# Linear attention, then a Fourier feed-forward: the first batch's loads, normalisation and the planner's durations rearranged

## The chip, the cores and the metric

The kernel runs on one core of a Trainium2 chip. The metric is device time in microseconds (us), the median of several executions. All data is 32-bit floating point; products that need the full width are made of three matmuls on a high and a low part.

## What is computed

There are 8 batches, 8 heads, 576 tokens and a head dimension of 64. The reference, cut to what matters:

```python
kv  = einsum('bhsd,bhse->bhde', k, v)
out = einsum('bhsd,bhde->bhse', q, kv)
out = out / sqrt(mean(out*out, -1) + 1e-6) * g_norm
x = out.transpose(0, 2, 1, 3).reshape(8, 576, 512)
u = x + real(fft(fft(x, axis=1), axis=2))
un = (u - mean(u)) / sqrt(var(u) + 1e-6)
return u + maximum(un @ w_ch1, 0) @ w_ch2     # 512 -> 2048 -> 512
```

The weights arrive as 64-bit numbers and are turned into pairs of 32-bit numbers on the chip.

## The kernel before, in words

The work is recorded as operations of a planner (class `Plan`), one after another, each with an engine, a duration in nanoseconds (its cost), a rank, the operations that it comes after, and the buffers that it needs. `Plan.run` plays this list against its own clock: of the ready operations on a free engine it emits the one with the lowest rank whose buffers are there. The order of emission becomes the order of the instructions on each engine, apart from a scheduler below it that moves instructions again. On the chip every engine takes its instructions strictly in that order. So a duration in the planner is no time on the chip, but it decides what stands behind what.

For every batch the plan holds these steps, and the names used in this document are theirs:

- **KV** (`plan_kv`, L441): keys and values are loaded by pairs of heads, 256 KB each for keys and values (`km`, `vm`, L460), with one remainder of 128 KB each (`kr`, `vr`, L469). Each pair costs 10 matmuls (L481). The ring `kv` holds 6 such tiles, so the fourth pair waits until the first pair's matmuls have released theirs.
- **QT** (`plan_q_load`, L497, and `plan_q`): the queries of a batch come in two loads of 576 KB (`qt`, L504: side 0 for the tokens of the first half, side 1 for the second half in mirrored order), and are transposed, 4 matmuls for each of 6 groups (L529). The token rows fall into three classes t = 0, 1, 2 (position modulo 3); class t needs a group of each side.
- **OUT** (`plan_out`): 16 matmuls per class (L554), then on ScalarE (ACT) a copy to `x` (L569) and a square (L574), on VectorE (DVE) a sum (L578), on GpSimd (POOL) a multiplication by `g_norm` (L589).
- **Inverse roots** (`plan_y`, L596): once per batch, for all three classes, a square root on ACT (L607), a reciprocal on DVE (L614), three refining steps on POOL (L618 to L620), a last product on DVE (L623).
- **Fold** (`plan_fold`, L632): on each class two multiplications by the inverse root (L651, DVE), one folding addition (L662, DVE), two on POOL (L669), a high part on ACT (L675) and a low part on POOL (L678). Its two work tiles `ab` and `xe` come from the ring `e2` with 4 places.
- **SEQ** (36 matmuls, L693), **CHN** (36, L727) and **TURN** (24 transposes, L813): the two Fourier steps as matmuls, with mixing on ACT, DVE and POOL between them, and the transposed result `unTh`, `unTl` (L822, L825).
- **F1** and **F2** (`plan_early`, L888; L354 and L372): the feed-forward. A block has 512 tokens. While the batches are prepared, F1 and F2 of the blocks that are ready fill TensorE (PE), with the first three of 16 chunks of the weights. An F1 of one chunk is 12 matmuls.
- **Weights** (`plan_w`, L835): one 512 KB load per chunk (`raw`, L282), a clearing step on ACT (L285), five bit steps on DVE (L292 to L302), a sum (L857), for the first matrix also a reduction (L307), a matmul for the mean (L315) and a subtraction (L319), then a high and a low part.

Everything is loaded by SyncE (SP), except the values of the first batch, whose loads are issued by ACT. At most eight loads are in flight: each load waits for the completion of the one eight places ahead of it (the semaphores `DMAHW0` to `DMAHW7` are handed out in turn). A load that waits holds up all that stand behind it on SP.

When the plan is finished, the remaining chunks and blocks follow in a loop that the change does not touch; there the order of PE's instructions is the same in both kernels.

## Time and profile before

| | us |
|---|---|
| median of 3 runs (1024.54 to 1029.22) | 1024.72 |
| the profiled execution | 1026.22 |
| its span, first to last instruction | 1024.4 |
| PE busy | 993.9 |
| DVE busy | 472.0 |
| ACT busy | 322.4 |
| POOL busy | 320.6 |

The profiled execution's time is 1.8 us above its span, and 1.5 us above the median. "Busy" is the time in which an engine works on an instruction; a load of weights into PE (PEld) overlaps its matmuls. PE is busy for 97% of the span, so the time left for it to lose or win is in the gaps and in how long one matmul takes. A row of a timeline shows the start and the length of a group of like instructions, and in brackets how long the engine was idle before it and what ended that.

### The profile page before, as it was taken

The page shows a single profiled execution, that of the slowest core. Times are in us where ns is not written, and L with a number is a line of the kernel's source. Part 1 is how long each engine was busy: PE and PEld are TensorE (multiplying, and loading weights), DVE is VectorE, ACT ScalarE, POOL GpSimd, SP SyncE. Part 2 cuts the span into 40 slices and gives each one's busy share as a digit, 9 for nine tenths or more (in the row PEclk, how much of TensorE's full clock was granted, in tenths as well). Part 3 has the DMA queues.
Part 4 walks back from the last instruction along what each step waited for, and adds up shares of the span by engine and source line. Part 5 has one row for each costly group of instructions (what it writes and reads, how often), then busy time and mean ns, then how long its engine had stood idle before and what let it go on. Part 6 is the DMA issues. An engine that isn't in the chain of part 4 may idle for free.

```text
span 1024.4 us, 15026 instructions
## 1 busy us (share of the span) xinstructions
PE 993.9 (97%) x5866; PEld 839.4 (82%) x5866; DVE 472.0 (46%) x838; ACT 322.4 (31%) x655; POOL 320.6 (31%) x332
## 2 busy tenths in 40 slices
PE   4698999999999999999999999999999999999998
PEld 4697898889888888888888888888888888888886
DVE  4758775654588689998131314131221311311211
ACT  2456565555545434334221212021121021210110
POOL 0555876864865131225722303020020010110000
PEclk9998999999999999999999999999999999999999
DMA  9979979663246766645552515140320400400101
GB/s 245 253 164 280 190 214 263 168 182 139 88 162 212 275 206 253 228 136 175 155 177 74 182 51 170 71 139 1 125 81 0 165 21 1 164 1 1 42 1 41
DMA packets 109194, 140.70 MB, mean 137 GB/s; under 512 B 51790, under 2 KB 76418, under 8 KB 104516
## 3 DMA queue, kind: packets, MB, share of 16 engines
q1 hardware_dynamic: 105588, 132.28, 42.4%
q0 software_dynamic: 1920, 6.29, 2.0%
q10 hardware_dynamic: 1616, 1.18, 0.4%
q8 instruction: 46, 0.75, 0.3%
q14 instruction: 24, 0.20, 0.1%
HBM read 88.33 MB, written 51.40 MB: 136 GB/s over the span
## 4 chain that ended last, share of the span: by engine, by line
PE 93%; DMA 2%; DVE 2%; SPq 1%; issue 1%; ACT 0%; POOL 0%; DVEq 0%; ACTq 0%; POOLq 0%
PE ps_h L354 38%; PE acc L372 38%; PE ps_o L554 4%; PE ps_f L727 3%; PE ps_f L693 3%; PE ps_k L481 3%; PE ps_q L529 2%; PE ps_t L813 2%; DMA vm<-in_v_dram 2%; DVE x L651 1%; DMA qt<-in_q_dram 1%; SPq L510 1%; PE ps_w L315 0%; SPq L460 0%; DVE unTl L825 0%
## 5 line engine op out<-in xcount | busy, mean ns | idle before, releaser
L354 PE MATMUL ps_h<-unTh,w 128*128 128x512 f32 x1152 | 357.1, 391 | 0.0
L372 PE MATMUL acc<-w,hh 128*128 128x512 f32 x1152 | 345.0, 391 | 0.2 <-DVE unTl L825 0.2
L367 DVE SCALAR_TENSOR_TENSOR hl<-ps_h,hh 128x512 fp32r<-128x512 f32 x144 | 99.2, 689 | 379.8 <-ACT hh L364 377.5
L354 PEld LDWEIGHTS ps_h<-unTh,w 128*128 128x128 f32 x1152 | 215.4, 188 | 44.0
L372 PEld LDWEIGHTS acc<-w,hh 128*128 128x128 f32 x1152 | 214.9, 188 | 44.3 <-issue 0.3
L364 ACT ACTIVATE hh<-ps_h 128x512 fp32r<-128x512 f32 x144 | 85.9, 597 | 472.1 <-PE ps_h L354 442.9
L354 PE MATMUL ps_h<-unTl,w 128*128 128x512 f32 x576 | 224.5, 390 | 0.0
L372 PE MATMUL acc<-w,hl 128*128 128x512 f32 x576 | 213.1, 390 | 0.0
L354 PEld LDWEIGHTS ps_h<-unTl,w 128*128 128x128 f32 x576 | 108.3, 188 | 22.7
L372 PEld LDWEIGHTS acc<-w,hl 128*128 128x128 f32 x576 | 107.9, 188 | 22.5
L1133 POOL DMA_INDIRECT uu<-u_scr,rowidx x24 | 23.4, 974 | 286.2 <-DVE uu L1186 175.6
L589 POOL TENSOR_TENSOR x<-x,gb 96x512 f32<-96x512 f32 (+1 forms) x48 | 61.9, 1308 | 55.2 <-ACT x L569 40.6
L1152 POOL TENSOR_TENSOR uu<-uu,up 128x512 f32<-128x512 f32 x36 | 45.7, 1293 | 44.5 <-ACT up L1149 44.5
L554 PEld LDWEIGHTS ps_o<-kvt,fq 64*96 64x96 f32 (+1 forms) x768 | 42.7, 185 | 5.6 <-issue 3.2
L554 PE MATMUL ps_o<-kvt,fq 64*96 64x64 f32 (+1 forms) x768 | 47.0, 274 | 0.3 <-ACT fq L533 0.3
L481 PE MATMUL ps_k<-vm,km 128*64 128x64 f32 x512 | 28.7, 261 | 17.6 <-DMA vm<-in_v_dram 16.7
L1096 POOL TENSOR_TENSOR w<-wap,w 128x512 fp32r<-128x512 f32 x18 | 23.3, 1295 | 70.1 <-ACT w L1095 70.1
L1186 DVE SCALAR_TENSOR_TENSOR uu<-acc,rs_yb,uu 128x512 f32<-128x512 f32 x36 | 25.2, 745 | 42.5 <-PE acc L372 42.5
L578 DVE TENSOR_REDUCE ss<-ps_o 96x8 f32<-96x512 f32 (+1 forms) x48 | 32.2, 682 | 26.2 <-ACT ps_o L574 26.0
L669 POOL TENSOR_TENSOR xe<-ab 96x256 f32<-96x256 f32 (+1 forms) x48 | 37.5, 803 | 19.8 <-DVE ab L662 19.7
L693 PE MATMUL ps_f<-cs,xh 96*128 96x290 f32 (+1 forms) x192 | 41.8, 312 | 0.4 <-DVE x L651 0.4
L481 PEld LDWEIGHTS ps_k<-vm,km 128*64 128x64 f32 x512 | 22.9, 166 | 22.4 <-DMA km<-in_k_dram 16.2
(103 smaller groups left out, 1009.1 us busy)
## 6 DMA issues: line engine op xcount, KB each, us to landing
raw<-in_moe_w_ch_dram SPq DMA_DIRECT2D x32, 512.0 KB, 7.6
qt<-in_q_dram SPq DMA_DIRECT2D x16, 576.0 KB, 9.2
unT_scr<-unTh SPq DMA_DIRECT2D x9, 1024.0 KB
unT_scr<-unTl SPq DMA_DIRECT2D x9, 1024.0 KB, 6.3
part_scr<-part SPq DMA_DIRECT2D x36, 256.0 KB, 4.1
unTh<-unT_scr SPq DMA_DIRECT2D x9, 1024.0 KB, 4.9
...
up<-part_scr SPq DMA_DIRECT2D x36, 256.0 KB, 3.0
```

The source lines that it names most:

```text
L354: nc.tensor.matmul(ps, w[c][:, kc * P : (kc + 1) * P], unT[a][:, kc, :], start=(idx == 0), stop=(idx == 3 * KC - 1),)
L364: nc.scalar.activation(hh, ps, AF.Relu)
L367: nc.vector.scalar_tensor_tensor(hl, ps, 0.0, hh.bitcast(F32), ALU.max, ALU.subtract)
L372: nc.tensor.matmul(acc, hpair[a][:, i * P : (i + 1) * P], w[c], start=(first and n == 0), stop=(last and n == 2),)
L481: nc.tensor.matmul(ps.t[s * D : (s + 1) * D, pr * D : (pr + 1) * D], km[:, s, j, :] if j < 4 else kr[:, h, :], vm[:, s, j, :] if j < 4 els ...
L554: nc.tensor.matmul(pss[s].t[:n, at : at + D], fqs[side].t[half, m, :n], kvt.t[half, m], start=True, stop=True,)
L578: nc.vector.tensor_reduce(ss.t[0][:n, :, t, s::2], pss[s].t[:n].rearrange("p (u m e) -> p u m e", u=2, e=D), AX.X, ALU.add,)
L589: nc.gpsimd.tensor_tensor(v_, v_, gb[:n].unsqueeze(1).to_broadcast([n, H, D]), ALU.mult)
L669: nc.gpsimd.tensor_tensor(o[:, s], a[:, 0], a[:, 1], ALU.subtract if s else ALU.add)
L693: nc.tensor.matmul(ps.t[:, :NS], xs[t].t[a][:n, part, ch * P : (ch + 1) * P], cs[:n, part, c, t, :], start=(idx == 0), stop=(idx == 8),)
L727: nc.tensor.matmul(ps.t[:n, :ND], pt.t[a][:, part, ch, offs[t] : offs[t] + n], cd[:, part, c, ch, :], start=(idx == 0), stop=(idx == 5),)
L1152: nc.gpsimd.tensor_tensor(us[j][i], us[j][i], part, ALU.add)
```

## The change

It does five things, nearly all for the first batch (b == 0).

1. The queries of the first batch come in six loads of 192 KB, by side and class, and each group of transposes waits for its own load only.
2. The inverse roots of the first batch are formed class by class (three times the six small steps, each on a third of the columns), and so class 0 needn't wait for class 2.
3. The last pair of keys and values of the first batch, and the last two pairs of the second, go to tiles of the feed-forward's ring `h`, which stands unused then, rather than to the ring `kv`. The fold of the first batch's class 2 takes its two work tiles from the ring `part`, which stands unused too.
4. The ranks of the weights' loads and conversions are set anew (`W_CONV`, `W_RANK`), so that they come later against the first batch.
5. The planner's durations are set anew: for KV, OUT and the parts of TURN, and every duration of PE counts double until three SEQ groups are done. `pin` ties the instructions that are emitted at the planner's time zero to their order.

The core of the diff, without the functions `pin` and the like:

```diff
+EARLY_KV = (1, 2)
+W_CONV = (4, 5, 6)
+W_RANK = (2, 4, 11)
...
+                    cost = o.cost * (2 if eng == "PE" and cold > 0 else 1)
+                    cold -= o.dense
...
+                if b < 2 and pr >= NPAIR - EARLY_KV[b]:
+                    main = Buf("h", lambda c=c: base.tile(
+                        [P, 2, 4, D], F32, name=c + "m", tag="r", bufs=RINGS["h"]
+                    ))
...
-            mm.append(op("PE", 520, rank(b, KV), go, ld + lds, [ps, kvt] + ts + rest))
+            mm.append(op("PE", 1080, rank(b, KV), go, ld + lds, [ps, kvt] + ts + rest))
...
+        if b == 0:
+            ld = [[dma(
+                240, rank(b, QT) + (2 - j if side else j) / 4,
+                lambda j=j: nc.sync.dma_start(
+                    qt.t[:TR, j].rearrange("p (h d) -> p h d", h=H), src[:, j]
+                ),
+                bufs=[qt],
+            )] for j in range(3)]
...
-        a = op("PE", 900, r, mm, done, [kvt, x, ss] + pss + fqs)
+        a = op("PE", 1540, r, mm, done, [kvt, x, ss] + pss + fqs)
...
-        ab, xe = e2_buf("ab"), e2_buf("xe")
+        if b == 0 and t == 2:
+            ab, xe = (Buf("part", part_tile) for _ in range(2))
+        else:
+            ab, xe = e2_buf("ab"), e2_buf("xe")
...
+        if b == 0:
+            ys = [plan_y(b, ss, reds[t] + [one_row], yp, t) for t in range(3)]
+        else:
+            ys = [plan_y(b, ss, sum(reds, []), yp)] * 3
...
-                    plan_w(which, f, lambda: wA, rank(0, FOLD) + f, [], (0, 3, 11)[f])
+                    plan_w(which, f, lambda: wA, W_CONV[f], [], W_RANK[f])
```

What this does to the order is seen at three places. In the changed file the lines have other numbers: KV loads L507 and L516 (were L460, L469), query loads L552 (L504), weights L322 (L282), KV L528 (L481), QT L585 (L529), OUT L610 (L554), the weights' mean L355 (L315).

The first loads on SP, before:

```order
L460 DMA km<-in_k_dram 128x2x256
L469 DMA kr<-in_k_dram 64x8x64
L460 DMA km<-in_k_dram 128x2x256 x2
L282 DMA raw<-in_moe_w_ch_dram 128x4x256
L460 DMA km<-in_k_dram 128x2x256
L282 DMA raw<-in_moe_w_ch_dram 128x1024
L412 DMA gb<-in_g_norm_dram 128x64
L504 DMA qt<-in_q_dram 96x24x64
L510 DMA qt<-in_q_dram 1x8x64
L504 DMA qt<-in_q_dram 96x24x64
```

and now:

```order
L507 DMA km<-in_k_dram 128x2x256
L516 DMA kr<-in_k_dram 64x8x64
L507 DMA km<-in_k_dram 128x2x256 x3
L452 DMA gb<-in_g_norm_dram 128x64
L552 DMA qt<-in_q_dram 96x8x64
L566 DMA qt<-in_q_dram 1x8x64
L552 DMA qt<-in_q_dram 96x8x64 x5
L322 DMA raw<-in_moe_w_ch_dram 128x4x256
L322 DMA raw<-in_moe_w_ch_dram 128x1024
```

The two loads of weights went behind all queries. Further on in SP's order all four pairs of the second batch's keys and values stand ahead of its queries; before, the fourth pair stood behind them.

PE from the first transposes on, before (`ps_q` is QT, `ps_o` OUT, `ps_k` KV, `ps_w` the weights' mean; a row of 97 is class 0):

```order
L529 MATMUL ps_q<-ident,qt 128x97 x4
L529 MATMUL ps_q<-ident,qt 128x96 x8
L315 MATMUL ps_w<-wp,mean_t 128x128
L529 MATMUL ps_q<-ident,qt 128x96 x4
L554 MATMUL ps_o<-kvt,fq 96x64 x8
L529 MATMUL ps_q<-ident,qt 128x96 x7
L554 MATMUL ps_o<-kvt,fq 96x64 x8
L529 MATMUL ps_q<-ident,qt 128x96
L554 MATMUL ps_o<-kvt,fq 96x64 x8
```

and now:

```order
L585 MATMUL ps_q<-ident,qt 128x97 x4
L585 MATMUL ps_q<-ident,qt 128x96 x12
L610 MATMUL ps_o<-kvt,fq 97x64 x16
L585 MATMUL ps_q<-ident,qt 128x96 x8
L610 MATMUL ps_o<-kvt,fq 96x64 x32
L528 MATMUL ps_k<-vm,km 64x64 x8
L528 MATMUL ps_k<-vr,kr 64x64 x2
L528 MATMUL ps_k<-vm,km 64x64 x8
L528 MATMUL ps_k<-vr,kr 64x64 x2
L355 MATMUL ps_w<-wp,mean_t 128x128
```

Class 0's OUT went ahead of the last two groups of QT, and the first weights' mean from the middle of QT to behind two pairs of the second batch's KV.

DVE up to the last step of the third chunk of the first matrix, `w_1066` before and `w_1169` now, which the third F1 needs (L578, now L634, is OUT's sum; L825 the low part of TURN; L651, now L710, the multiplication by the inverse root; L662, now L721, the folding addition). Before:

```order
L825 TENSOR_TENSOR unTl<-ps_t,unTh 128x4x75
L319 TENSOR_TENSOR wa<-wa,ps_w 128x512
L825 TENSOR_TENSOR unTl<-ps_t,unTh 128x4x96
L578 TENSOR_REDUCE ss<-ps_o 96x2x4
L825 TENSOR_TENSOR unTl<-ps_t,unTh 128x4x21
L825 TENSOR_TENSOR unTl<-ps_t,unTh 128x4x74
L578 TENSOR_REDUCE ss<-ps_o 96x2x4
L866 TENSOR_TENSOR w_1066<-wa,w_1066 128x512
```

and now:

```order
L407 SCALAR_TENSOR_TENSOR hl<-ps_h,hh 128x512
L710 TENSOR_TENSOR x<-x,ps_y 97x512 x2
L710 TENSOR_TENSOR x<-x,ps_y 96x512 x4
L721 TENSOR_TENSOR ab<-x 97x512
L634 TENSOR_REDUCE ss<-ps_o 96x2x4
L721 TENSOR_TENSOR ab<-x 96x512
L634 TENSOR_REDUCE ss<-ps_o 96x2x4
L359 TENSOR_TENSOR wa<-wa,ps_w 128x512
L634 TENSOR_REDUCE ss<-ps_o 97x2x4 x2
L332 TENSOR_SCALAR ps_a<-ps_a 128x512
L926 TENSOR_TENSOR w_1169<-wa,w_1169 128x512
```

This step went behind the second batch's six multiplications; before, it stood ahead of them.

More of the change, by code (lines that the diff above doesn't have):

```diff
@@ L37 @@
 PAD_RIGHT = 224
+EARLY_KV = (1, 2)
+W_CONV = (4, 5, 6)
+W_RANK = (2, 4, 11)
+PIN_UNTIL = 0
+PINNED = {
+    mybir.EngineType.PE, mybir.EngineType.DVE, mybir.EngineType.Activation,
+    mybir.EngineType.Pool, mybir.EngineType.SP,
+}
 RINGS = {
@@ L67, with __init__ @@
     AHEAD = 4000
-    def __init__(self, rings):
+    def __init__(self, rings, tc=None):
+        self.tc, self.last = tc, {}
+        self.pinned = PINNED
         self.rings = dict(rings)
@@ L91, in dma, with pin @@
         return o
+    def pin(self, emit, now):
+        tc = self.tc
+        traced = tc.nc.cur_bb.bb.instructions
+        start = len(traced)
+        emit()
+        traced = tc.nc.cur_bb.bb.instructions
+        for i in traced[start:]:
+            if i.engine not in self.pinned or now > PIN_UNTIL:
+                continue
+            last = self.last.get(i.engine)
+            if last:
+                tc.add_manual_dep(
+                    i, last,
+                    mybir.DependencyInfo(
+                        mybir.DependencyClass.NoSync, mybir.DependencyReason.DATA
+                    ),
+                    reason="the plan's order",
+                )
+            self.last[i.engine] = i.name
     def run(self):
@@ L109, in run @@
         port = 0
+        cold = 3
         left = len(self.ops)
@@ L151, in run @@
                             b.t = b.make() or True
-                    o.emit()
-                    self.trace.append((t, t + o.cost, eng, o))
-                    end = free[eng] = t + o.cost
+                    self.pin(o.emit, t)
+                    cost = o.cost * (2 if eng == "PE" and cold > 0 else 1)
+                    cold -= o.dense
+                    self.trace.append((t, t + cost, eng, o))
+                    end = free[eng] = t + cost
                     if o.port:
@@ L591, in scale, with plan_y, of, sums @@
                 )
-            gs.append(op("POOL", 1300, r, scale, cs_ + [i_gb], [x]))
+            gs.append([op("POOL", 1300, r, scale, cs_ + [i_gb], [x])])
         return ds, gs
-    def plan_y(b, ss, reds):
-        n = TR + 1
-        w = 6 * H
-        yp = bank_buf("ps_y")
-        def flat(a):
-            return a[:n].rearrange("p s t h -> p (s t h)")
+    def plan_y(b, ss, reds, yp, t=None):
+        n = TR + 1 if t is None else rows[t]
+        ts = slice(None) if t is None else slice(t, t + 1)
+        def of(a):
+            return a[:n].rearrange("p (s t h) -> p s t h", s=2, t=3)[:, :, ts]
+        def sums():
+            return ss.t[0][:n, :, ts]
         def root():
-            ss.s = two.tile([P, w], F32, name="rs_s")
-            nc.scalar.activation(ss.s[:n], flat(ss.t[0]), AF.Sqrt, scale=1.0 / D, bias=eps_t[:n])
+            nc.scalar.activation(of(ss.t[2]), sums(), AF.Sqrt, scale=1.0 / D, bias=eps_t[:n])
         def mean():
-            nc.gpsimd.tensor_scalar(ss.t[1][:n], flat(ss.t[0]), 1.0 / D, EPS, ALU.mult, ALU.add)
+            nc.gpsimd.tensor_scalar(of(ss.t[1]), sums(), 1.0 / D, EPS, ALU.mult, ALU.add)
         def recip():
-            ss.y0 = two.tile([P, w], F32, name="rs_y")
-            nc.vector.reciprocal(ss.y0[:n], ss.s[:n])
+            nc.vector.reciprocal(of(ss.t[3]), of(ss.t[2]))
         def refine():
-            t, y = ss.s[:n], ss.y0[:n]
-            nc.gpsimd.tensor_tensor(t, y, ss.t[1][:n], ALU.mult)
-            nc.gpsimd.tensor_tensor(t, t, y, ALU.mult)
-            nc.gpsimd.tensor_scalar(t, t, -0.5, 1.5, ALU.mult, ALU.add)
+            t_, y = of(ss.t[2]), of(ss.t[3])
+            nc.gpsimd.tensor_tensor(t_, y, of(ss.t[1]), ALU.mult)
+            nc.gpsimd.tensor_tensor(t_, t_, y, ALU.mult)
+            nc.gpsimd.tensor_scalar(t_, t_, -0.5, 1.5, ALU.mult, ALU.add)
         def last():
-            nc.vector.tensor_tensor(yp.t[:n, :w], ss.y0[:n], ss.s[:n], ALU.mult)
+            nc.vector.tensor_tensor(of(yp.t[:, : 6 * H]), of(ss.t[3]), of(ss.t[2]), ALU.mult)
         r = rank(b, SCL)
@@ L651, in mul @@
                 nc.vector.tensor_tensor(v_, v_, y.unsqueeze(2).to_broadcast([n, H, D]), ALU.mult)
-            ms.append(op("DVE", 690, r, mul, [y_done, gs[s]], [x, yp]))
+            ms.append(op("DVE", 690, r, mul, [y_done] + gs[s], [x, yp]))
         def zero():
@@ L828, in low @@
                 )
-            h = op("ACT", 180 + 3 * (hi - lo), r, high, [a], [ps, unTs[j]])
-            turned[j] += [h, op("DVE", 180 + 4 * (hi - lo), r, low, [h], [ps, unTs[j]])]
+            h = op("ACT", 180 + 5.6 * (hi - lo), r, high, [a], [ps, unTs[j]])
+            turned[j] += [h, op("DVE", 180 + 5.3 * (hi - lo), r, low, [h], [ps, unTs[j]])]
     w_done = {}
@@ L939 @@
         ss = Buf("two", lambda: (
-            two.tile([P, 2, 3, H], F32, name="ss"), two.tile([P, 6 * H], F32, name="m")
+            two.tile([P, 2, 3, H], F32, name="ss"),
+            *[two.tile([P, 6 * H], F32, name=c) for c in ("m", "rs_s", "rs_y")],
         ))
@@ L949 @@
             for j in range(3):
-                fqs[side, 2 - j if side else j] = plan_q(b, side, j, qt, loaded)
+                fqs[side, 2 - j if side else j] = plan_q(b, side, j, qt, loaded[j])
         for t in range(3):
@@ L956 @@
             )
-            reds += d
-        y, yp = plan_y(b, ss, reds)
+            reds.append(d)
+        yp = bank_buf("ps_y")
+        if b == 0:
+            ys = [plan_y(b, ss, reds[t] + [one_row], yp, t) for t in range(3)]
+        else:
+            ys = [plan_y(b, ss, sum(reds, []), yp)] * 3
         if b == 0:
```

28 lines of the change are left out of this document (17 added, 11 removed).

## The prediction, made before the changed kernel ran

> **What bounds the kernel now.** I read the page's first lines, then who waited for whom on TensorE, then the stretches, then the timelines of the first 110 us, engine by engine.
>
> ```profile
> PE 993.9 (97%) x5866; PEld 839.4 (82%) x5866; DVE 472.0 (46%) x838; ACT 322.4 (31%) x655; POOL 320.6 (31%) x332
> PE ps_k L481 <- DMA vm<-in_v_dram: 16.7, 4, 8.3
> ...
> 0.00:10.00 10.00, 2.71 (x38) 2.31 (x38) 0.25 (x3) 1.49 (x2) 0.91 (x8) 1.00 0.83 238
> 40.00:50.00 10.00, 4.61 (x42) 4.18 (x42) 6.57 (x11) 2.39 (x7) 3.60 (x4) 1.00 1.12 282
> 50.00:60.00 10.00, 10.00 (x108) 8.62 (x108) 5.11 (x9) 6.03 (x13) 7.65 (x8) 1.00 1.17 173
> ...
> 120.00:140.00 20.00, 20.00 (x171) 18.19 (x170) 10.80 (x24) 12.86 (x33) 18.32 (x18) 1.00 0.60 169
> ```
>
> PE is the bound: busy for 993.9 us, 97% of the span. Its longest waits are for loaded values, and lie in the first stretches (columns: PE, PEld, DVE, ACT, POOL, granted clock, DMA share, GB/s): 2.71 and 4.61 us busy of 10. From 120 us on it is full. So the change can win only in the first 110 us, and what it wins there comes off the end. The places:
>
> ```profile
> 4.62 1.12 PE L481 MATMUL ps_k<-vm,km 128*64 128x64 f32 x16 [4.62 <-DMA vm<-in_v_dram]
> 7.66 0.48 PE L481 MATMUL ps_k<-vr,kr 64*64 64x64 f32 x4 [1.91 <-DMA vr<-in_v_dram]
> 8.89 1.12 PE L481 MATMUL ps_k<-vm,km 128*64 128x64 f32 x16 [0.76 <-DMA vm<-in_v_dram]
> 12.77 1.12 PE L481 MATMUL ps_k<-vm,km 128*64 128x64 f32 x16 [0.89 <-DMA km<-in_k_dram]
> 18.86 2.16 PE L529 MATMUL ps_q<-ident,qt 97*128 97x97 f32 x12 [4.55 <-DMA qt<-in_q_dram]
> 21.80 0.90 PE L529 MATMUL ps_q<-ident,qt 96*128 96x96 f32 x4 [0.29 <-DMA qt<-in_q_dram]
> 27.25 5.50 PE L554 MATMUL ps_o<-kvt,fq 64*96 64x64 f32 x64
> 45.39 1.12 PE L481 MATMUL ps_k<-vm,km 128*64 128x64 f32 x16 [8.27 <-DMA vm<-in_v_dram]
> 46.86 2.83 PE L529 MATMUL ps_q<-ident,qt 97*128 97x97 f32 x16
> 60.64 0.85 PE L693 MATMUL ps_f<-cs,xh 97*128 97x290 f32 x2
> 68.19 1.59 PE L554 MATMUL ps_o<-kvt,fq 64*97 64x64 f32 x32
> 71.80 4.52 PE L727 MATMUL ps_f<-cd,pt 128*97 128x258 f32 x36
> 76.16 1.15 PE L529 MATMUL ps_q<-ident,qt 96*128 96x96 f32 x12
> 80.88 0.69 PE L481 MATMUL ps_k<-vm,km 128*64 128x64 f32 x16
> 81.75 0.69 PE L481 MATMUL ps_k<-vm,km 128*64 128x64 f32 x16
> 82.63 0.88 PE L813 MATMUL ps_t<-ident,x 96*128 96x96 f32 x8
> 91.99 1.12 PE L481 MATMUL ps_k<-vm,km 128*64 128x64 f32 x16 [3.03 <-DMA vm<-in_v_dram]
> 95.34 1.20 PE L354 MATMUL ps_h<-unTh,w 128*128 128x512 f32 x2
> 108.99 0.73 PE L354 MATMUL ps_h<-unTh,w 128*128 128x512 f32 x2
> ```
>
> (The profile counts each OUT and KV matmul twice.) PE also runs at two speeds. 16 OUT take 2.75 us at 27 us (half of 5.50) and 1.5 to 1.59 at 68; 10 KV take 1.47 from 45.39 to 46.86 and 0.87 from 80.88 to 81.75. The switch comes inside SEQ, and after 3.03 us of idle KV is slow again (1.12 for 0.69).
>
> **The change, part by part.** I follow PE to one point, the end of the third F1, after which it has fillers in both kernels.
>
> *The loads.* Rates, from two stretches of two us and the issues:
>
> ```profile
> 8.00:10.00 2.00, 1.24 (x21) 1.02 (x18) 0.00 (x0) 0.00 (x0) 0.00 (x0) 1.00 1.09 350
> 16.00:18.00 2.00, 0.00 (x0) 0.00 (x0) 1.93 (x4) 0.00 (x0) 0.00 (x0) 1.00 0.99 170
> qt<-in_q_dram SPq DMA_DIRECT2D x10, 576.0 KB, 9.2
> km<-in_k_dram SPq DMA_DIRECT2D x20, 256.0 KB, 5.3
> 12.44 0.70 DVE L292 TENSOR_SCALAR ps_a<-ps_a 128x512 f32<-128x512 f32 x1 [11.38 <-ACT ps_a L285]
> ```
>
> Keys, values and weights move at about 340 GB/s, queries alone at 170. The first keys and values are 2.36 MB, at 238 GB/s in by 10 us; PE's first KV (from 4.62, four times 1.47 and the waits of 1.91 and 0.76, which remain) ends near 13.2 instead of 14.2; the 0.89 for the fourth pair goes, since its tiles needn't be released first. Queries: 1.18 MB at 170 GB/s, 6.9 us, all in by 17 (before by 21.8, behind 1.05 MB of weights); four of six pieces by 14.6. QT and OUT of the first batch need 12.5 us at the slow rate (2.83 + 1.4 + 8.25), start at 13.2 and end at 25.6, where before they ended at 32.7. Then in SP's order: weights 1.05 MB to 20, the Fourier constants 0.93 MB, at the 240 to 280 GB/s of a mixed stretch, to 23.7, the second batch's keys and values 2.36 MB to 30.6. Its KV ends at 33 rather than 47. Then 0.79 MB to 33, a side of queries to 36.5, 0.5 MB of weights to 38, the other side to 41.5. So PE idles about 3.5 and 2.7 us there, in place of 8.27. After 41.5: 4 QT, 8 OUT, 8 QT, 8 OUT, 20 KV, 0.7 + 1.4 + 1.4 + 1.4 + 2.9 = 7.8 us. SEQ starts at 49.3 instead of 60.6.
>
> [...] The traces show the overlap: 256 KB loads take 5.3 us to land and yet move 350 GB/s.
>
> *Is the fold ready at 49.3?* Before:
>
> ```profile
> 40.53 3.67 DVE L651 TENSOR_TENSOR x<-x,ps_y 97x512 f32<-97x512 f32 x6
> 46.71 1.20 DVE L662 TENSOR_TENSOR ab<-x 96x512 f32<-96x512 f32 x1 [1.30 <-POOL xe L669]
> 46.97 0.37 ACT L492 COPY kvt<-ps_k 128x256 f32<-128x256 f32 x1 [8.73 <-PE ps_k L481]
> 52.58 1.41 POOL L669 TENSOR_TENSOR xe<-ab 96x256 f32<-96x256 f32 x2
> 55.38 2.49 POOL L589 TENSOR_TENSOR x<-x,gb 96x512 f32<-96x512 f32 x2 [0.16 <-ACT x L569]
> 57.84 1.26 POOL L678 TENSOR_TENSOR xl<-xe,xh 96x512 fp32r<-96x512 f32 x1
> ```
>
> ACT stood 8.73 us at the copy of `kvt` with the high parts behind it; with KV at 33 that goes. The 1.30 us for a free `xe` go with the two slots. The last sum comes 6 to 7 us earlier with OUT; two bit steps and a low part stand ahead of the multiplications; I put these at 35.3, and the folds at 40 to 43. POOL then has six `xe` (4.2 us), three `xl` (3.8) and, between them, two `gb` multiplications of batch 1 (2.5) that wait for OUT at 46.2: its last `xl` ends at 52.6. The SEQ order takes all of class 0 first and class 2 last, so PE isn't held. SEQ, at 7.55 us as before (60.64 to 68.19), plus a mean and two KV, ends at 57.5.
>
> *The small steps.* Three times the roots adds 4 instructions on DVE, 8 on POOL, 2 on ACT.
>
> ```profile
> L614 DVE RECIPROCAL rs_y<-rs_s 97x48 f32<-97x48 f32 x8 | 3.6, 446 | 0.8 <-ACT rs_s L607 0.8
> ```
>
> Each works on a third of the columns, so one costs between a third of 0.446 us and all of it: 0.6 to 1.8 us on DVE; I take 1.2, the middle, since no row shows how much of it is fixed. All lie before 35 us. DVE then idles until PE's second mean inside SEQ, near 54, which covers them; without it they would cost their 1.2. `h` and `part` slots are free again at 33 and 53, long before the first F1: nothing.
>
> *From SEQ to the first F1* PE has 16 OUT, 36 CHN, 9 KV, 16 OUT, 9 KV, 16 QT, 16 TURN, 30 KV, 8 TURN, 16 OUT, 8 QT: at the fast rate 4.5 for OUT, 4.4 CHN, 4.2 KV, 2.3 QT and 2.5 TURN, 17.9 us, to 75.4, and about 1.3 for the fourth batch's remainders, which SP issues behind the first store of `u`: 76.7. Before it was 95.34.
>
> *VectorE then ends last.* The weights stand behind the queries, so DVE's first bit step comes at about 18.8, not 12.44. From the second mean (54.5) to `w_1169` its new order has 34 instructions of full width, at the pitch of the next two rows (0.60), the six multiplications (3.6) and 20 smaller ones of about 0.43 (as the reciprocal): 20.4 + 3.6 + 8.6 = 32.6 us.
>
> ```profile
> 90.09 0.67 DVE L866 TENSOR_TENSOR w<-wa,w 128x512 fp32r<-128x512 f32 x1
> 90.69 0.68 DVE L292 TENSOR_SCALAR ps_a<-ps_a 128x512 f32<-128x512 f32 x1
> ...
> 70.00:100.00 30.00, 26.68 (x350) 23.76 (x348) 25.30 (x47) 20.36 (x49) 18.50 (x20) 0.89 0.91 261
> ```
>
> Packed, that ends at 87.1; at DVE's share of the third row (25.3 of 30, 84%), 38.8 us, at 93.3. Packed, PE runs from 76.7 through F1, 32 OUT, mean, KV, QT, F1, QT and the third F1, ending at 90.4. At 84% the third F1 waits and ends at 96.0. Before it ended at 111.7 (108.99 + 2.73), with 30 KV, 12 QT and 32 OUT more behind it, 2.6 + 1.2 + 3.0 = 6.8 us. So 96.0 compares with 102.8: **8.9 us won**; packed, 14.5. I take 8.9, since that share is measured.
>
> The profiled execution took 1026.22, span and 1.8; 8.9 less is 1017.3. It lies 1.5 above the median of 1024.72, to which my number belongs: 1015.8. A measurement of this kernel can tell about 0.5%, 5.1 us, from no change.
>
> **Rivals.**
> *Packed.* DVE's gaps close: 14.5 us won, 1010.2. For it: the batches' sums come earlier. Against: the share above, with 4.7 us of gaps in 30.
> *An earlier fast speed.* If unbroken work of PE before SEQ were enough, the 7.8 us after 41.5 would shrink as KV does (0.87 for 1.47) by some 3.2, and 12.1 would be won: 1012.6. Against: PE is full from 50 to 60 us and still slow when SEQ begins (0.85 for two, 60.64). [...]
> *DVE takes it back.* If its share after 54.5 is 70%, its 32.6 us take 46.6 and the third F1 ends at 103.8, or 110.6 compared: 1.1 won, 1023.6. Below 76% less than 5.1 us are left. For it: most of its instructions wait for a partner on ACT or PE; against: what it waits for comes earlier.
> *Pieces don't overlap.* Should the six land two at a time at 5.3 us, queries are in at 26, not 17: nothing is won, 1024.7. Against: eight are in flight.
> *Slower: a ring of waits.* PE's third mean stands ahead of KV, QT and two F1, and waits for DVE, whose order holds batch sums that wait for PE's OUT. If that puts DVE at 60%, 54.3 us, the third F1 ends at 111.5, compared 118.3: 6.6 us lost, 1031.3. PE would slow down as well, as after its 3.03 us of idle. It decides below about 68%.
>
> **How the numbers follow.** Forecast (5.1 to 12 us won) 0.58; packed 0.12; an earlier fast speed 0.03; DVE takes it back 0.17, a tenth of it still over 5.1; pieces 0.05; slower 0.05. Faster 0.73 + 0.02 = 0.75, same 0.20, slower 0.05. From 1009.5 to 1022.0 lie the forecast, three quarters of packed (0.09), the earlier speed and seven tenths of the case in which DVE takes it back (0.12): 0.82.
>
> **What would show it.** Right: OUT of the first batch ends near 25.6; two PE waits for `qt` between 33 and 42; SEQ near 49; first F1 near 77; third F1 near 93, waiting for `w`. Wrong: queries landing after 20, SEQ waiting for `xl`, a PE idle of 3 us or more after 57 with slow matmuls behind it, or waits on PE after 110.

## The result: slower, 1033.15 us against 1026.73

On the same chip the changed kernel takes 1033.15 us (median of 8 executions, 1027.85 to 1036.41) and the kernel before 1026.73 (8 executions, 1024.54 to 1029.22). The ratio is 1.0062, with a 95% interval from 1.0043 to 1.0080: some 6 us slower, where 9 us faster was forecast. Its eight executions follow their mean granted clock: those at 0.985 to 0.988 take 1033.0 to 1036.4, those at 0.993 to 0.994 take 1027.9 to 1031.8. The profiled one is a long one (1036.41, span 1034.6, clock 0.985), so its trace shows 10.2 us more of span than the trace of before.

The page's first line, in the changed kernel:

```profile
PE 1004.1 (97%) x5866; PEld 847.3 (82%) x5866; DVE 469.9 (45%) x842; ACT 323.0 (31%) x657; POOL 324.7 (31%) x340
```

PE is busy 1004.1 us, before 993.9: 10.2 us more with the same 5866 matmuls. Its idle time is 30.5 us in both (1034.6 less 1004.1, 1024.4 less 993.9). So nothing of the loss is waiting as such; the same work took longer. The stretches say where (columns as before: length, PE, PEld, DVE, ACT, POOL, granted clock, DMA share, GB/s), first of the changed kernel:

```profile
60.00:78.00 18.00, 16.32 (x200) 14.72 (x199) 16.08 (x31) 12.42 (x32) 11.56 (x10) 1.00 0.58 169
78.00:79.00 1.00, 0.53 (x6) 0.44 (x8) 1.00 (x2) 0.52 (x2) 0.92 (x2) 0.64 1.15 177
79.00:88.00 9.00, 9.00 (x83) 8.03 (x84) 4.75 (x10) 1.99 (x5) 1.46 (x6) 0.50 1.01 262
88.00:95.00 7.00, 7.00 (x26) 5.46 (x26) 1.50 (x3) 2.28 (x5) 2.50 (x2) 0.50 1.04 382
96.00:102.00 6.00, 4.97 (x86) 4.28 (x84) 5.55 (x8) 5.10 (x13) 3.70 (x3) 1.00 0.61 140
102.00:109.00 7.00, 4.09 (x10) 3.22 (x11) 7.00 (x9) 2.19 (x5) 5.19 (x7) 0.51 0.32 74
185.00:190.00 5.00, 5.00 (x32) 3.96 (x31) 3.35 (x5) 3.09 (x7) 2.52 (x2) 0.50 1.23 268
```

and of the kernel before its one such stretch:

```profile
90.00:97.00 7.00, 5.01 (x36) 4.51 (x37) 6.97 (x13) 4.54 (x11) 2.49 (x2) 0.52 0.96 332
```

PE works at half clock for 16.9 us from 78.3 on, for 4.1 of the 6.8 us from 102.2 and for 6.8 from 184.1, 27.8 us in all; before, for 5.0 of the 6.8 us from 90.2. Half of the difference is 11.4 us; in turn PE's slow work at the start, up to its first fast matmul in SEQ, is 43.6 us and was 45.0, which gives 0.7 back. (The clock's column reads 1.00 there; that PE was slow is read from the durations: two SEQ matmuls take 0.69 us at 54.42 and 0.43 at 61.58.) Together 10.7 us, beside the loss of 10.2. PE's timeline of the changed kernel at the places that the prediction spoke of (start, length, engine, line, operation, tiles, count, idle time before it and what ended it):

```profile
26.07 2.83 PE L610 MATMUL ps_o<-kvt,fq 64*96 64x64 f32 x32 [1.66 <-ACT fq L589]
39.95 2.16 PE L585 MATMUL ps_q<-ident,qt 96*128 96x96 f32 x12 [4.07 <-DVE ps_a L332]
45.38 0.88 PE L585 MATMUL ps_q<-ident,qt 96*128 96x96 f32 x4 [3.27 <-DMA qt<-in_q_dram]
53.53 0.85 PE L752 MATMUL ps_f<-cs,xh 97*128 97x290 f32 x2
75.87 0.69 PE L528 MATMUL ps_k<-vm,km 128*64 128x64 f32 x16
78.47 0.48 PE L528 MATMUL ps_k<-vr,kr 64*64 64x64 f32 x4 [1.92 <-DMA vr<-in_v_dram]
78.89 1.12 PE L528 MATMUL ps_k<-vm,km 128*64 128x64 f32 x16
87.55 1.54 PE L585 MATMUL ps_q<-ident,qt 96*128 96x96 f32 x8
88.80 1.20 PE L394 MATMUL ps_h<-unTh,w 128*128 128x512 f32 x2
104.91 1.22 PE L394 MATMUL ps_h<-unTh,w 128*128 128x512 f32 x2 [3.59 <-DVE ss L634]
183.88 0.34 PE L528 MATMUL ps_k<-vr,kr 64*64 64x64 f32 x4 [1.49 <-DMA vr<-in_v_dram]
```

The lead is there: SEQ starts at 53.5, 7.1 us ahead of the 60.64 of before. Then PE waits 1.92 us for the fourth batch's `vr`; behind that wait a group of KV takes 1.12 us where the same took 0.69 ahead of it, 8 QT take 1.54 where they take 0.88, and it lasts until 95.3, 6.5 us into the first F1. Waits of 3.59 and 1.49 us are followed by the same. SyncE's queue shows why `vr` was late:

```profile
57.73 0.46 SPq L507 DMA_DIRECT2D vm<-in_v_dram  x1
67.31 0.34 SPq L322 DMA_DIRECT2D raw<-in_moe_w_ch_dram  x1
68.21 0.45 SPq L507 DMA_DIRECT2D vm<-in_v_dram  x1
71.76 0.69 SPq L828 DMA_DIRECT2D u_scr<-x  x2
74.22 0.62 SPq L516 DMA_DIRECT2D vr<-in_v_dram  x1
```

A load of weights stands until 67.31 for a tile that DVE frees (9.0 us of that wait are put down to `wp`, L342), then the first store of `u` until 71.76 for POOL's `x`; `vr` follows at 74.22. DMA moves 169 GB/s from 60 to 78, after 242 up to 53.5. In the kernel before, SP issued this load at 72.57 and PE came to it at 81.49:

```profile
72.57 0.63 SPq L469 DMA_DIRECT2D vr<-in_v_dram  x1
81.49 0.33 PE L481 MATMUL ps_k<-vr,kr 64*64 64x64 f32 x4
```

Now PE came to it at 76.55, 4.9 us earlier, and the load was issued 1.65 us later.

### The profile page after: what moved, and what is told of

It reads as the page before. It is cut to its first block, busy times and chain, and to the rows that moved or that the text cites. A ratio compares the mean times of both kernels' runs of the same rounds, so it can differ in the third digit from the quotient of the medians.

```text
span 1034.6 us, 15049 instructions
## 1 busy us (share of the span) xinstructions
PE 1004.1 (97%) x5866; PEld 847.3 (82%) x5866; DVE 469.9 (45%) x842; ACT 323.0 (31%) x657; POOL 324.7 (31%) x340
## 4 chain that ended last, share of the span: by engine, by line
PE 93%; DMA 4%; DVE 1%; SPq 1%; issue 0%; ACT 0%; ACTq 0%; DVEq 0%
PE ps_h L394 38%; PE acc L412 38%; PE ps_f L752 4%; PE ps_f L787 3%; PE ps_o L610 3%; PE ps_k L528 2%; PE ps_t L873 2%; PE ps_q L585 1%; DMA vr<-in_v_dram 1%; DMA draw<-in_dft_s_dram 1%; DMA qt<-in_q_dram 1%; DMA vm<-in_v_dram 1%; DMA draw<-in_dft_d_dram 1%; DMA km<-in_k_dram 0%; PE ps_w L355 0%
## 5 line engine op out<-in xcount | busy, mean ns | idle before, releaser
L610 PEld LDWEIGHTS ps_o<-kvt,fq 64*96 64x96 f32 (+1 forms) x768 | 44.8, 187 | 7.4 <-issue 4.0
L610 PE MATMUL ps_o<-kvt,fq 64*96 64x64 f32 (+1 forms) x768 | 49.0, 276 | 1.7 <-ACT fq L589 1.7
L634 DVE TENSOR_REDUCE ss<-ps_o 96x8 f32<-96x512 f32 (+1 forms) x48 | 32.1, 682 | 22.4 <-ACT ps_o L630 22.1
L1205 DVE BATCH_NORM_STATS2 bst<-uu 128x6 f32<-128x512 f32 x36 | 24.6, 689 | 27.6 <-DMA uu<-u_scr,rowidx 17.8
L787 PE MATMUL ps_f<-cd,pt 128*96 128x258 f32 (+1 forms) x288 | 36.6, 283 | 0.0
```

The lines of the kernel that those rows point to most:

```text
L610: nc.tensor.matmul(pss[s].t[:n, at : at + D], fqs[side].t[half, m, :n], kvt.t[half, m], start=True, stop=True,)
L634: nc.vector.tensor_reduce(ss.t[0][:n, :, t, s::2], pss[s].t[:n].rearrange("p (u m e) -> p u m e", u=2, e=D), AX.X, ALU.add,)
L787: nc.tensor.matmul(ps.t[:n, :ND], pt.t[a][:, part, ch, offs[t] : offs[t] + n], cd[:, part, c, ch, :], start=(idx == 0), stop=(idx == 5),)
```

## Experiments

My theory after the trace: a wait of PE costs more than its length, since the granted clock falls with it (to 0.50 here, behind 1.92 us) and comes back only some microseconds into the next F1 (6.5 and 4.1 here); and the early lead is given back to later waits for loads. Rivals: the slow matmuls have another cause; the new durations or ranks are at fault; the lead itself is worth its length. In the kernels with added matmuls PE does work whose result is overwritten. Each set below ran on one chip, beside the kernel before.

**First set: what the clock costs.** Added to the changed kernel, ahead of the fourth batch's first KV:

```diff
+                if (b, pr) == (3, 0):
+                    for _ in range(18):
+                        nc.tensor.matmul(
+                            ps.t[:, 256:512], cs[: TR + 1, 0, 0, 0, :P],
+                            cs[: TR + 1, 0, 0, 0, :256], start=True, stop=True,
+                        )
```

> The changed kernel with 18 matmuls of 97x128 by 256 that nobody reads, ahead of the fourth batch's first KV, where TensorE idled 1.92 us for the remainders of its values and then ran at half clock from 78.4 to 94.6 us. Clock theory (the wait lets the clock fall, and the slow 16 us cost about 8): the wait is filled, the granted clock stays at 1.00 from 72 to 95 us, the first F1 comes near 84 instead of 88.8, and the time falls by 6 to 9 us, to within 0.2% of the kernel before. Rival, low activity: the short matmuls of KV, QT, OUT and TURN from 72 to 84 us let it fall in any case; the clock falls all the same and the time stays within 2 us of the changed kernel or above it. Rival, late weights: nothing is gained, since VectorE holds the second F1.

1026.89 us, ratio 1.0022 (1.0000 to 1.0045). The stretch of 78 to 95 us in the changed kernel, then in this one, and this one's first F1 and its longest later wait:

```profile
78.00:95.00 17.00, 16.53 (x111) 13.93 (x112) 7.24 (x14) 4.79 (x11) 4.88 (x9) 0.51 1.03 306
```

```profile
78.00:95.00 17.00, 14.72 (x219) 12.40 (x219) 14.62 (x27) 10.40 (x25) 9.81 (x13) 1.00 0.98 273
```

```profile
83.97 0.72 PE L394 MATMUL ps_h<-unTh,w 128*128 128x512 f32 x2
101.37 0.52 PE L591 MATMUL ps_q<-ident,qt 96*128 96x96 f32 x4 [3.31 <-DMA qt<-in_q_dram]
```

With the wait filled the clock stays at 1.00, 219 matmul records are done in 14.7 us where 111 took 16.5, and F1 starts at 83.97, 4.8 us earlier although 2.4 us of work were added. At the end the loss against the kernel before has shrunk from 0.62% to 0.22%, some 4 us (6.3 between the medians of the two sets), where 6 to 9 were expected. PE is then early for the next load (3.31 us), its clock falls there for 3.4 us, and the kernel only comes level with before.

The fourth batch's remainders in the ring `part`, so that their loads needn't wait for the ring `kr`:

```diff
+            if b == 3:
+                kr = Buf("part", lambda c=c: base.tile(
+                    [P // 2, H, D], F32, name=c + "r", tag="part", bufs=RINGS["part"]
+                ))
...
```

> The changed kernel with the fourth batch's remainders of keys and values in the two slots of the ring part, so that their loads needn't wait for the third batch's KV and don't stand behind the first store of u. Clock theory: the wait of 1.92 us is gone, the clock stays at 1.00 up to the second F1, and the time falls by 7 to 10 us (8 for the clock, 2 for the wait). Low activity: the wait goes, the clock falls all the same, 2 us at most are won. Late weights: 2 us at most.

1028.25, ratio 1.0022 (1.0007 to 1.0038): again some 4 us won, where 7 to 10 were expected. The wait at 78 shrinks to 0.62 and the clock holds; it falls at 96 behind waits of 0.59 and 1.08 us for DVE, and at 103 behind 1.06 for `qt`.

The old ranks of the weights, and the old durations:

```diff
-                    plan_w(which, f, lambda: wA, W_CONV[f], [], W_RANK[f])
+                    plan_w(which, f, lambda: wA, rank(0, FOLD) + f, [], (0, 3, 11)[f])
```

> The changed kernel with the ranks of the weights' loads and conversions as before. Late weights theory: the wait of 3.59 us before the second F1 and the slow clock behind it go, and the time falls by 5 to 10 us below the changed kernel. Clock theory: the time depends on whether a wait of 2 us or more falls into the stretch from 70 to 110 us; if the granted clock falls there as long as in the changed kernel, the time stays within 2 us of it.

```diff
-        cold = 3
+        cold = 0
...
-            mm.append(op("PE", 1080, rank(b, KV), go, ld + lds, [ps, kvt] + ts + rest))
+            mm.append(op("PE", 520, rank(b, KV), go, ld + lds, [ps, kvt] + ts + rest))
...
-        a = op("PE", 1540, r, mm, done, [kvt, x, ss] + pss + fqs)
+        a = op("PE", 900, r, mm, done, [kvt, x, ss] + pss + fqs)
...
```

> The changed kernel with the planner's durations as before (KV, OUT, TURN, and no doubling at the start). If the new durations are what spoils the order from 70 to 110 us, the time falls to the kernel before or below; if they are not, it stays within 3 us of the changed kernel or rises. Clock theory: in either case the difference to the changed kernel is the difference in TensorE's slow time after 66 us, about half of it.

Old ranks: 1028.82, ratio 1.0039 (1.0021 to 1.0057); the fourth batch's last `vm` is waited for instead (4.06 us at 92.28) and the clock falls there. Old durations: 1037.39, ratio 1.0118 (1.0089 to 1.0148), with half the clock from 77.7 to 101.6 and, inside that, 4.89 us of waiting for `vr` up to 83.82. The new durations help; the ranks move the wait.

**Second set: what the lead is worth.** A second filling, 36 matmuls of 97x128x128, went in front of the QT that waited 3.31 us:

```diff
+            if (b, side, j) == (3, 1, 0):
+                for _ in range(36):
+                    nc.tensor.matmul(
+                        ps.t[:, 384:512], cs[: TR + 1, 0, 0, 0, :P],
+                        cs[: TR + 1, 0, 0, 0, :P], start=True, stop=True,
+                    )
```

> The changed kernel with two sets of added matmuls whose results are overwritten: 18 of 97x128x256 ahead of the fourth batch's first keys and values (as in the run with one set, 1026.9), and 36 of 97x128x128 between the high parts of F1 and the QT that waited 3.31 us for qt at 101.37 there. Clock theory: the granted clock is 1.00 in every stretch from 60 to 120 us, the matmuls behind that QT take the fast duration (F1 0.62 for two, not 1.05), about 2 us less of PE's busy time, 1024 to 1025. Loads theory: qt lands no earlier, so QT still starts at about 101 and nothing but those 2 us can go. Rival (added work costs what it saves): 1026.5 to 1027.5.

In the trace the clock is at 1.00 from 60 to 120 as expected; the time is not: 1029.27, ratio 1.0030 (1.0016 to 1.0043), above all three expectations. The traced execution is the fastest of the ten, 1026.81 with a mean clock of 0.998; the others have 0.993 to 0.997, and where their clock fell isn't on record. The 36 matmuls take 4.2 us, the two fillings some 1.4 more than the waits that they fill, and waits for DVE (1.66 at 93.12, 1.12 at 98.69) remain. So even the execution whose clock held through that stretch isn't ahead of before's 1026.35; without the 1.4 us it would be at an estimated 1025.4, 1 us ahead.

The same was tried in the kernel before, with 26 matmuls ahead of the KV that waited 3.03 us:

```diff
+                if (b, pr) == (3, 3):
+                    for _ in range(26):
+                        nc.tensor.matmul(
+                            ps.t[:, 256:512], cs[: TR + 1, 0, 0, 0, :P],
+                            cs[: TR + 1, 0, 0, 0, :256], start=True, stop=True,
+                        )
```

> The kernel before with 26 added matmuls of 97x128x256, overwritten afterwards, ahead of the fourth batch's last pair of keys and values, where PE waits 3.03 us for vm at 91.99. Clock theory: the granted clock, 0.50 to 0.61 from 90 to 97 us before, stays 1.00, and about 3 us go: 0.997 of before, some 1023. Then the kernel before, with its one cold stretch filled, is at least as fast as the changed one with its two filled, and the change brings nothing by itself. Rival (slow matmuls after the wait have another cause): 1.000 and the same low clock at 91 to 97.

Inconclusive: 1028.09, ratio 1.0015 (0.9990 to 1.0039). They ran too early, from 87.41 to 90.79; a wait of 1.89 us was left and the clock fell from 92.5 to 99.5.

Two parts of the change undone, each on top of the two fillings:

```diff
-        if b == 0:
+        if b < 0:
             ys = [plan_y(b, ss, reds[t] + [one_row], yp, t) for t in range(3)]
```

> As the changed kernel with two sets of added matmuls, but with the first batch's inverse roots taken at once, as before the change. PE's order is the same. If the class roots give an earlier fold (the prediction had them free of cost and the multiplications at 35), SEQ starts 3 us or more later than in the kernel with roots by class (53.3 there) and the time is 1 to 3 us longer. If the fold is set by what ACT and DVE do meanwhile for the Fourier constants (2.92 us at 23.72 and 2.61 at 35.69 of ACT's waits for them), SEQ starts within 1.5 us of it and the time is within 1 us.

```diff
-        if b == 0:
+        if b < 0:
             ld = [[dma(
                 240, rank(b, QT) + (2 - j if side else j) / 4,
```

> As the changed kernel with two sets of added matmuls, but the first batch's queries are loaded a whole side at a time, as before the change; the plan then puts KV of the second batch in other places too. The pieces let QT start at 15.2 instead of 18.9: without them OUT of the first batch ends about 4 us later, at 32 to 33, and SEQ starts at 56 to 58. If an early lead reaches the end (the prediction), the time is 3 to 5 us longer; if it is given back to later waits for loads, it is within 1.5 us, with the waits for qt and vm shorter by what the lead is less.

SEQ's first matmuls with everything changed, with roots at once, and with whole queries:

```profile
52.13 0.85 PE L764 MATMUL ps_f<-cs,xh 97*128 97x290 f32 x2
```

```profile
53.09 0.85 PE L764 MATMUL ps_f<-cs,xh 97*128 97x290 f32 x2
```

```profile
56.27 0.85 PE L764 MATMUL ps_f<-cs,xh 97*128 97x290 f32 x2
```

The times: 1029.27; 1028.68, ratio 1.0021 (1.0006 to 1.0036); 1029.20, ratio 1.0041 (1.0017 to 1.0065). In the six kernels of this document with the changed head and roots by class (the changed one, four with added matmuls or other remainders, and the one with the stores on ACT, below) SEQ starts between 51.83 and 53.99. The 53.09 with roots at once lies inside, as the second of its expectations has it; the 56.27 with whole queries is 2.3 to 4.4 us later. Neither is seen at the end. The lead is real, and it is given back.

**Third set: the loads alone.** In the first kernel the stores of `u` leave SP for ACT's queue; the other three stand for the kernel before with only the query pieces, only the slots for keys and values, and both. They are made from the changed file by undoing the rest of the change, except `pin`.

```diff
-            dma(kb, r, lambda: nc.sync.dma_start(dst, src()), adds, [x])
+            dma(kb, r, lambda: nc.scalar.dma_start(dst, src()), adds, [x], eng="ACT")
```

> The changed kernel with the stores of u issued by ACT instead of SP, so that on SP nothing waits for POOL's x ahead of the fourth batch's keys and values (km, kr and vr were issued at 72.98 to 74.22, behind a store that waited until 71.76). The plan orders PE's work from 70 us on anew with it. Clock theory: if the wait for vr at 78.47 goes, the granted clock stays 1.00 from 78 to 95 and some 6 to 8 us go, 1026 to 1027. Rival: ACT, in order, now stands for POOL's x with evictions behind it; PE waits for ACT over 1 us somewhere between 70 and 110, its clock falls there, and the time is 1030 or more.

1031.48, ratio 1.0070 (1.0044 to 1.0096). `vr` is no longer waited for, but the plan now puts a mean of the weights in its place, and the clock is at half from 77 to 94:

```profile
82.07 0.77 PE L355 MATMUL ps_w<-wp,mean_t 128*128 128x128 f32 x2 [6.33 <-DVE wp L347]
```

> The kernel before with the first batch's queries loaded by classes of rows, and nothing else of the change (its plan then orders the work anew). Lead theory, the prediction's: QT starts near 15 instead of 18.86, SEQ 3 us or more before 60.6, and that stays to the end: 0.997. Theory that loads give it back: QT starts near 15, but the second batch's keys and values land no earlier, so the wait of 8.27 us at 45.39 grows by what was won and SEQ starts within 1.5 us of before; 0.999 to 1.003, more if a wait of over 1 us between 60 and 110 lets the clock fall for longer than before's 7 us.

> The kernel before with the last keys and values of the first two batches in slots of the feed-forward, and nothing else of the change. Lead theory: the wait of 8.27 us at 45.39 shrinks by 3 us or more, SEQ starts at 55 to 58, and the time falls with it: 0.996 to 0.997. Theory that later waits take it: SEQ earlier by the same, but waits for loads between 62 and 110 us grow by as much, 0.999 to 1.003; the state of the clock there (full or half from 78 to 97) decides the rest.

> The kernel before with both loads changed, queries by classes and the slots for keys and values; roots at once, fold, ranks of the weights and the plan's durations as before the change. Lead theory: SEQ starts 5 to 7 us before 60.6 and 0.993 to 0.996 results. Theory that later waits take it: the lead is there at SEQ and gone at the third F1, 0.999 to 1.003. If it is below 0.997, it is the new durations, the roots or the ranks that turned the loads' gain into a loss; if not, the loads are what gives it back.

| before with | SEQ from | first F1 | us | ratio |
|---|---|---|---|---|
| nothing | 60.64 | 95.34 | 1026.11 | 1 |
| query pieces | 57.87 | 92.01 | 1033.68 | 1.0078 (1.0056 to 1.0099) |
| slots | 62.33 | 91.87 | 1023.84 | 0.9982 (0.9965 to 0.9998) |
| both | 56.94 | 91.06 | 1032.50 | 1.0049 (1.0025 to 1.0072) |

The part that gives the lead is the part that loses, and the one that wins a little, against both expectations, gives no lead at all: with the slots SEQ is 1.7 us later, but the wait for the fourth batch's `vm` is gone. (Its clock falls all the same, from 90.6 to 97.4, behind a wait of 0.85 us for DVE.) With both parts the ten executions fall in two groups: three with a mean clock of 0.996 or more take 1025.9 to 1026.3, seven at 0.990 or less 1031.8 to 1034.2. The traced one, of the second group, is at half clock from 82.4 to 96.1 and from 106.3 to 113.1. So the falls are worth about 7 us, and the three executions whose clock hardly fell are level with before: there the two loads are worth nothing. None of the three kernels came out in a range that was stated for it, unless the clause on the clock is counted.

With the pieces alone the clock fell twice: at 107.4, behind a wait of 2.57 us for a weight, and before that where PE waited for nothing. PE's timeline and stretches there:

```profile
80.21 0.45 PE L528 MATMUL ps_k<-vm,km 128*64 128x64 f32 x6
80.59 1.57 PE L610 MATMUL ps_o<-kvt,fq 64*96 64x64 f32 x16
82.09 0.45 PE L528 MATMUL ps_k<-vm,km 128*64 128x64 f32 x8
```

```profile
76.00:82.00 6.00, 6.00 (x94) 5.25 (x93) 5.96 (x9) 4.69 (x11) 6.00 (x8) 1.00 0.84 175
82.00:84.00 2.00, 2.00 (x25) 1.86 (x25) 2.00 (x5) 1.16 (x2) 2.00 (x2) 0.87 0.90 260
84.00:97.00 13.00, 13.00 (x88) 10.96 (x88) 8.70 (x18) 6.80 (x15) 6.34 (x10) 0.50 1.03 260
```

No idle time from 76 to 83, and half the clock from 83.5 to 97.1. That put the wait itself in question: a stretch of short matmuls might be enough.

**Fourth set: wait or short matmuls.** In the changed kernel the place of the wide added matmuls is taken by 28 of the shape of a KV step:

```diff
+                if (b, pr) == (3, 0):
+                    for _ in range(28):
+                        nc.tensor.matmul(
+                            ps.t[:D, 256:320], ident[:, :D], ident[:, :D],
+                            start=True, stop=True,
+                        )
```

> The changed kernel with 28 added matmuls of the shape of a KV step (128x64 by 128x64, plain f32), overwritten afterwards, ahead of the fourth batch's first keys and values, where 18 wide ones (97x128x256) stood in the run that kept the clock. They take about 2.4 us, as the wide ones did, so PE has no wait over 0.5 us at 78. If the wait makes the clock fall: it stays 1.00 from 78 to 88 and the time is 1026 to 1028, as with the wide ones. If a stretch of short matmuls does, waits or not: the clock falls between 77 and 82 all the same, stays at 0.50 until some 6 us after the first F1, and the time is 1032 to 1036.

1028.43, ratio 1.0026 (1.0000 to 1.0051). The added matmuls and the KV behind them, and the stretch:

```profile
74.33 3.42 PE L527 MATMUL ps_k<-ident 128*64 128x64 f32 x55
78.47 0.69 PE L534 MATMUL ps_k<-vm,km 128*64 128x64 f32 x16
```

```profile
78.00:95.00 17.00, 14.76 (x211) 12.47 (x208) 13.79 (x25) 10.13 (x23) 9.04 (x13) 0.97 1.01 322
```

The 28 (two records each) take 3.3 us, up to 77.64, rather than 2.4. The clock holds to 94 us and F1 starts at 83.19. Short matmuls fill the wait as well as wide ones: in the changed kernel the wait was the cause. In the kernel with both loads the same two fillings, `range(18)` wide or `range(28)` short, went ahead of the fourth batch's second pair, `(b, pr) == (3, 1)`:

> The kernel before with both loads changed (1032.5, or 1026 in the three of ten executions whose mean clock was over 0.995), with 18 added matmuls of 97x128x256, overwritten afterwards, ahead of the fourth batch's second pair of keys and values, where PE waits for nothing. If short matmuls make the clock fall: it no longer falls at 82, all executions are near 1026 to 1028, and none has a mean clock of 0.990 or less. If waits make it fall: nothing waits there, so the added work costs its 2.4 us, 1033 to 1036.

> As the run with wide matmuls at the fourth batch's second pair of keys and values, but with 28 of the shape of a KV step in their place, the same 2.4 us. If short matmuls make the clock fall: the clock falls at 79 to 84 and stays at 0.50 longer than without them, since the first F1 comes 2.4 us later: 1033 to 1037, or 1028 in executions in which it doesn't fall. If any added work keeps the clock: 1026 to 1028.

1035.62, ratio 1.0097 (1.0069 to 1.0126), and 1034.14, ratio 1.0078 (1.0056 to 1.0099). Each time lies in a range that was stated, the first for waits and the second for short matmuls as the cause, but neither came about in the way that was stated with it. With either filling the clock no longer falls at 82; PE goes on at 1.00 until it meets the fourth batch's last `vm`, here in the wide and then the short filling:

```profile
89.65 0.69 PE L534 MATMUL ps_k<-vm,km 128*64 128x64 f32 x16 [2.87 <-DMA vm<-in_v_dram]
```

```profile
89.27 0.69 PE L534 MATMUL ps_k<-vm,km 128*64 128x64 f32 x16 [2.02 <-DMA vm<-in_v_dram]
```

Behind these waits it is at half the clock from 90.5 or 90.6 to 101. With short fillings PE had done nothing but short matmuls since 72.9, 14 us at full clock up to the wait, so these alone didn't bring the clock down here. The last run fills the slots' kernel in the same way, 14 wide ones at `(3, 2)`:

> The kernel before with the slots for keys and values alone (1023.84, ratio 0.9982, its clock at 0.50 from 90.5 to 97.5 us), with 14 added matmuls of 97x128x256, overwritten afterwards, ahead of the fourth batch's third pair of keys and values, some 8 us before the first F1. If wide matmuls keep the clock through the stretch: 0.9955 to 0.997 of before, the added 1.9 us paid by 3 to 3.5 us of the clock and a wait of 0.85. If they don't: 0.9995 to 1.001.

1030.10, ratio 1.0046 (1.0029 to 1.0063), slower than either expectation: a wait of 1.94 us for `vm` at 91.88 takes the place of the 0.85, and the clock falls from 93 to 100. Added work makes nothing faster than the slots alone, the only version here below before, by less than the 0.5% that one measurement can tell.

## Why the prediction was wrong

The mechanism of the first 50 us was largely right, the price of one wait was not, and what the lead would be worth at the end was not either. Point by point, from PE's view:

*Loads and pieces: right.* The queries were in by 20; OUT of the first batch ended at 28.9, not 25.6, 1.66 of it a wait for ACT's `fq`; KV of the second batch ended at 35.9, not 33; the two waits ahead of QT ended at 39.95 and 45.38, and were 4.07 and 3.27 us long where 3.5 and 2.7 stood. (The view puts the first down to DVE's `ps_a`, and only the second to queries.) The rival in which pieces don't overlap fell. SP issued the pieces from 7.61 to 13.98 us, and PE waited 0.39 us for them in all.

*SEQ at 49.3: late by 4.2.* It started at 53.5, for the second side of the queries let PE go on at 45.38, not 41.5, and the work up to SEQ took 8.15 us, not 7.8; PE had no wait in between, so the fold didn't hold it.

*The fold ready at 49.3: late, without a price.* The last `xl` ran until 59.74, not 52.6, and PE didn't wait for it. I followed the class sums through DVE and POOL, and left out that ACT stands 2.92 and 2.61 us at the conversions of the Fourier constants, waiting for their loads:

```profile
23.72 0.93 ACT L471 ACTIVATE cs<-draw 97x870 fp32r<-97x870 f32 x1 [2.92 <-DMA draw<-in_dft_s_dram]
35.69 0.63 ACT L471 ACTIVATE cd<-draw 128x516 fp32r<-128x516 f32 x1 [2.61 <-DMA draw<-in_dft_d_dram]
```

with copies of `x` behind them, and DVE behind ACT:

```profile
36.36 0.70 DVE L474 TENSOR_TENSOR cd<-draw,cd 128x516 fp32r<-128x516 f32 x1 [2.99 <-ACT cd L471]
43.03 3.67 DVE L710 TENSOR_TENSOR x<-x,ps_y 97x512 f32<-97x512 f32 x6
```

The multiplications came at 43.03, not 35.3. In the six kernels with this head ACT's last conversion starts between 34.12 and 35.69, and the multiplications follow it by 7.33 or 7.34 us each time. That ties them to it, though no run moved the conversion by itself. With roots at once they follow by 7.36 us: roots by class gave nothing here. On DVE they cost 0.7 us more, three reciprocals and products of 0.71 and 0.61 us in all for one each of 0.44 and 0.20.

*From SEQ to the first F1: the step that failed.* It said "about 1.3 for the fourth batch's remainders, which SP issues behind the first store of `u`". The wait was found, in the right place and nearly of the right length (1.92), and was priced as idle time. Its price was the clock: F1 started at 88.80, 26.2 us behind SEQ's end at 62.6, where the sum had 19.2; of these 7.0 us, 5.2 are half of the 10.3 between 78.5 and F1, and the first 6.5 of F1 were slow as well. I had quoted the row that shows the effect, 3.03 us of idle with KV at 1.12 behind it, and took it for a threshold of about three. 1.92 and 1.49 us were enough, and in the slower rival I put the slowing beside a wait of DVE alone.

Length alone doesn't sort these waits: 1.02 us was followed by half clock in one place, 1.66 wasn't in another (the list at the end has both). So I looked at where a wait lies. The stretches at half clock are 17.07, 6.83 and 6.83 us long in the changed kernel, 6.83 before (90.22 to 97.04), and in the other traces, up to 112 us, where both ends are on record, between 3.41 and 23.90; each is a whole number of times 3.41 us (one to seven), within 0.03. I divided the time from 66 to 112 us at this step, counted from a fall, in the seventeen traces in which the place of a fall is on record (all but that with roots at once), and call a step a beat. Of the 144 beats at full clock whose successor is on record too, all 14 in which PE was busy for 0.51 of it or less were followed by half clock, 5 of the 13 between 0.52 and 0.82, and 2 of the 117 above that. Those two are in the kernels with the query pieces alone and with both loads, between 79.0 and 83.5 us, where PE was busy throughout. Of the wait of 1.92 us, 1.72 lay in one beat, from 74.86 to 78.27, and PE was busy for 0.50 of it.

In the changed kernel ten us of KV, QT, TURN and OUT from 78.5 to 88.8 didn't bring the full clock back, where 4.1 us of F1 did from 104.91 on.

The price here is thus set by what follows the wait. Before, the fall came at 90.2, 5 us ahead of F1, and cost 2.5 us; here 10.5 us ahead, and 8.4.

*VectorE last, the third F1 at 96.0: late by 16.7.* It ended at 112.7: 4.2 us from SEQ's start, 7.9 up to F1, and 4.6 behind that, with 3.59 us of waiting for DVE. There DVE's addition took 3.62 us where the next took 0.83:

```profile
100.64 3.62 DVE L721 TENSOR_TENSOR ab<-x 97x512 f32<-97x512 f32 x1
```

POOL worked at its `gb` multiplications meanwhile (5.40 us from 98.30); whether that held it up wasn't tried. And DVE had come late to all of this, since it stood 5.20 us for the first F1, which was slow:

```profile
96.45 0.69 DVE L407 SCALAR_TENSOR_TENSOR hl<-ps_h,hh 128x512 fp32r<-128x512 f32 x1 [5.20 <-ACT hh L404]
```

The wait was ahead of the second F1, for a batch sum. For `w` the third F1 didn't wait: it was ready at 109.2. So of the rivals the slower one came nearest, with its third F1 at 111.5 and 1031.3 us, but PE's third mean, on which it was built, came at 98.58 without a wait; the nearness of its time is in part luck. Compared (6.8 us of work), 119.5 against 111.7: 7.8 lost, not 8.9 won.

*What the lead is worth.* Even with the clock held, the 8.9 would not have come. PE's longest wait of before was for loads, and the loads of the fourth batch land where they did: its last `vm` ends a wait between 89.3 and 92.7 in before, with the old ranks and in four kernels with fillings. A PE that is early meets them earlier. I had said that the change can win only what PE waits in the first 110 us, and then gave it a lead without asking whether the loads from 60 to 90 move up too. They don't: SP stands 9.0 us for DVE (up to 67.31) and 3.0 for POOL (up to 71.76) of the time from 58 to 72. The rival of an earlier fast speed fell: PE was busy from 46.2 without a wait and still slow at 53.53 (0.85).

What stays open: why the clock fell at 83 us with the pieces alone. The OUT there are 8 in 1.57 us, not 0.90, and no view shows why. That such slow OUT have the effect of a wait is argued, not shown. For it speak the kernel with the old durations, here in the first row, whose clock fell at 77.7 behind such OUT and a wait of only 0.61 us, and the slots' kernel, with 2.92 us of such OUT and a wait of 0.85. Against it speaks the kernel with other remainders, in the second row, whose clock held:

```profile
73.72 2.99 PE L610 MATMUL ps_o<-kvt,fq 64*96 64x64 f32 x32
81.32 2.64 PE L617 MATMUL ps_o<-kvt,fq 64*96 64x64 f32 x32
```

Open too is how much of the spread between executions of one kernel comes from where a wait lies against the beat.
